# Reading the moving operand of the MLP matmuls in pairs of 64-byte pieces, with the weights at eight places

## The chip, the core and the metric

The kernel runs on one core of a Trainium2 chip. The metric is the time of one execution on the device in microseconds (us). TensorE (PE) multiplies a stationary operand of 128 columns, which a weight load (PEld) brings in, with a moving operand that streams past it, and sums in PSUM. VectorE (DVE) and ScalarE (ACT) read PSUM and write SBUF.

## The reference

An attention with exponential features and then two MLPs over 2304 tokens, one after the other, each 512 to 2048 to 512:

```python
q_p, k_p = (phi(q), phi(k))
...
attn_out = (num / den)
x = np.ascontiguousarray(attn_out.transpose(0, 2, 1, 3)).reshape(B * S, H * D)
h = x @ moe_w_in;  g = np.maximum(0.01 * h, h);             x = g @ moe_w_out
h = x @ moe2_w_in; g = h * np.tanh(np.log1p(np.exp(h)));    x = g @ moe2_w_out
```

(`phi` projects with `w_phi`, subtracts the largest absolute value and takes `exp` of both signs; the softplus of the second MLP is cut at 20.)

## The kernel before

The attention comes first, sixteen pairs of heads one after the other. It leaves X, the transposed activations, in SBUF. Then each MLP runs over five blocks of tokens: two of 512, the 256 left-over tokens, and two more of 512. The function `moe` works on a list `seq` of steps; one step is one block and one 128-wide slice `m` of the hidden layer (two slices for the block of 256 tokens). Sixteen slices `m` make the hidden layer.

In a step, `emit_h` makes the hidden values: four chunks `kk` of the model dimension are summed into a PSUM bank `a`. `leaky` or `mish` turn that bank into the activated values on ACT and DVE, and `emit_o`, two or three steps later, multiplies them into four banks `b`.

Every product is made of three matmuls in the function `three` (lines 83 to 86). A number is split into a high part and a low part, both of type fp32r: high by high, high by low, low by high. Each of the three has a weight load of its own, and the next load runs while the current matmul streams.

What moves and what stays differs by place. In `emit_h` the weights of slice `m` stay (tiles `wh`, `wl` of slice m, part 0) and a window of the activations moves (tiles `wh`, `wl` of the pool `winp`; the trace gives both kinds the same name). In `emit_o` of the first MLP the output weights stay (part 1 of the same tiles) and the activated values `gh`, `gl` move. In `emit_o` of the second MLP it is the other way: 128 columns of `gh` or `gl` stay, and the output weights move. The moving operand is a contiguous stretch of 512 or 256 columns of 4 bytes in each partition, read from the first to the last, and so is the output in PSUM.

Where the tiles lie matters here. The pools stand in SBUF one behind the other. `X` takes 36,864 bytes of a partition and `two` 32, and all tiles of the MLPs behind them have sizes that are multiples of 512 bytes. So every moving and every stationary operand of both MLPs starts at the same place modulo 512, namely 160 bytes past a multiple of 512 (the offsets of chunks and slices are multiples of 512 bytes too). A stationary operand of 128 columns is 512 bytes of each partition.

The order of the instructions is written out by hand (`tc.manual_schedule()`).

Of the kernel before, what the change touches and what calls it, by code (L numbers as in the profile page):

```python
# [10 lines left out]
F32 = mybir.dt.float32  # L11
# [12 lines left out]
def attention_two_mlps_kernel(  # L24
# [17 lines left out]
    P = 128  # L42
    KD = DM // P
    M = DFF // P
# [17 lines left out]
    xp = tc.alloc_tile_pool(name="xp", bufs=1)  # L62
# [7 lines left out]

    X = xp.tile([P, KD, NT], F32, name="X")
    two = xp.tile([P, 1], F32, name="two")[:, 0:1]

    rings = {"a": ps}

    def bank(ring):
        return rings[ring].tile([P, 512], F32, tag=ring, name=ring)
# [2 lines left out]
        nc.scalar.activation(out=hi, in_=src, func=AF.Copy)  # L80
        nc.vector.tensor_tensor(out=lo, in0=src, in1=hi.bitcast(F32), op=ALU.subtract)

    def three(o, wh_, wl_, xh, xl, start=True, stop=True):
        nc.tensor.matmul(out=o, lhsT=wh_, rhs=xh, start=start, stop=False)  # L84
        nc.tensor.matmul(out=o, lhsT=wh_, rhs=xl, start=False, stop=False)  # L85
        nc.tensor.matmul(out=o, lhsT=wl_, rhs=xh, start=False, stop=stop)  # L86
# [6 lines left out]
    class Conv:  # L93
# [45 lines left out]
        def split(self):  # L139

            if self.half is not None:
                u, c = self.half
                self.half = None
                split_w(self.which, u // 2, u % 2, c)()
# [25 lines left out]
        def step(self, *between):  # L170
# [3 lines left out]
            if self.open is not None:  # L174
                u, kind, c, e = self.open
                if kind != "fetch":
                    nc.vector.scalar_tensor_tensor(out=c.bitcast(I32), in0=c.bitcast(I32), scalar=3, in1=e,
                                                   op0=ALU.logical_shift_left, op1=ALU.bitwise_or)
                if kind == "store":
                    scr[self.which, u] = dr.tile([P, DM], F32, name=f"scr{self.which}_{u}")  # L180
                    nc.sync.dma_start(out=scr[self.which, u], in_=c)
                else:
                    after = split_w(self.which, u // 2, u % 2, c)
# [25 lines left out]
    def split_w(which, m, x, src):  # L209

        if x == 0:
            pool = wp0 if m < EARLY else wp
            W[which, m] = [pool.tile([P, 2, KD, P], F32R, tag=f"{t}{m}", name=f"w{t}{m}") for t in "hl"]
        hi, lo = (t[:, x].rearrange("p k f -> p (k f)") for t in W[which, m])
        nc.scalar.activation(out=hi, in_=src, func=AF.Copy)
        return lambda: nc.vector.tensor_tensor(out=lo, in0=src, in1=hi.bitcast(F32), op=ALU.subtract)
# [19 lines left out]
    def split_w2(m, parts=(0, 1)):  # L236
        for x in parts:
            split_w(1, m, x, w_st.pop((m, x)))()
# [12 lines left out]
    with tc.manual_schedule():  # L251
# [112 lines left out]
        def k_proj(i, c):  # L364
            s = st[i]
            if c == 0:
                s["kd"] = ap.tile([P, 2, NM, F], F32, tag="kd", name="kd")
            t = bank("a")
            for j in range(2):
                u = slice((2 * c + j) * P, (2 * c + j + 1) * P)  # L370
                three(t[:, j * 2 * F:(j + 1) * 2 * F], s["kh"][:, u], s["kl"][:, u], wbh, wbl)
            k_guard(t.rearrange("p (n f) -> p n f", f=F), NM, s["kd"][:, c])

        def k_proj_left(i):
            l = lf[i // 2]
            l["kd"] = ap.tile([P, 2, F], F32, tag="kdl", name="kdl", bufs=1)
            t = bank("a")
            three(t[:, 0:2 * F], l["h"][:, 0:P], l["l"][:, 0:P], wbh, wbl)
            k_guard(t[:, 0:2 * F].rearrange("p (n f) -> p n f", f=F), 2, l["kd"])
# [6 lines left out]
        def q_proj(i, c):  # L386
            s = st[i]
            h, o = divmod(c, 2)
            if "qd" not in s:
                s["qd"] = ap.tile([P, 2, S], F32, tag="qd", name="qd")  # L390
                s["qm"] = ap.tile([P, 2, S], F32, tag="qm", name="qm", bufs=1)
            t = bank("a")
            n = HM + (h == o) * LEFT
            c0 = h * (HM + (1 - o) * LEFT)
            d0 = (1 - o) * (HM + h * LEFT)
            f = slice(o * F, (o + 1) * F)
            three(t[:, 0:n], wbh[:, f], wbl[:, f], s["qh"][:, c0:c0 + n], s["ql"][:, c0:c0 + n])
            nc.scalar.activation(out=s["qd"][:, h, d0:d0 + n], in_=t[:, 0:n], func=AF.Copy)  # L398
            half = s.setdefault("half", set())
            half.add(c)  # L400
            if {2 * h, 2 * h + 1} <= half:
                qd, qm = s["qd"][:, h, :], s["qm"][:, h, :]
                nc.gpsimd.partition_all_reduce(qm, qd, P, bass_isa.ReduceOp.absmax)  # L403
# [176 lines left out]
        def emit_h(it):  # L580
            j, ms = it
            a, c0, n = blocks[j]
            hb[it] = bank("a")
            for i, m in enumerate(ms):
                hi, lo = W[a, m]
                for kk in range(KD):
                    three(hb[it][:, i * n:(i + 1) * n], hi[:, 0, kk, :], lo[:, 0, kk, :], win[j][kk][0], win[j][kk][1],
                          start=(kk == 0), stop=(kk == KD - 1))

        def emit_o(it, ds=None):  # L590
            j, ms = it
            a, c0, n = blocks[j]
            gh, gl = gt[it]
            nb = KD if a == 0 else n // P
            if ms[0] == 0:
                acc[j] = [bank("b") for _ in range(nb)]
            for d in ds or range(nb):
                for i, m in enumerate(ms):
                    hi, lo = (x[:, 1] for x in W[a, m])
                    if a == 0:  # L600
                        c = slice(i * n, (i + 1) * n)
                        three(acc[j][d][:, 0:n], hi[:, d, :], lo[:, d, :], gh[:, c], gl[:, c],
                              start=(m == 0), stop=(m == M - 1))
                    else:
                        c = slice(i * n + d * P, i * n + (d + 1) * P)
                        three(acc[j][d], gh[:, c], gl[:, c], hi.rearrange("p k f -> p (k f)"),
                              lo.rearrange("p k f -> p (k f)"), start=(m == 0), stop=(m == M - 1))

        def finish(j, d):
            a, c0, n = blocks[j]  # L610
# [102 lines left out]
        def moe(g):  # L713
            for x in [g, g + 1] if g == jump else [g + 1] if g > jump else [g]:
                if x < len(seq):
                    if x != HEAD:
                        emit_h(seq[x])
                    if seq[x][1][-1] == M - 1 and seq[x][0] + 1 < NB:
                        window(seq[x][0] + 1)
# [13 lines left out]
            if 0 <= g - 2 < len(seq) and seq[g - 2][0] <= last1:  # L733
                j, ms = seq[g - 2]
                emit_o(seq[g - 2])
                if ms[-1] == M - 1:
                    for d in range(KD):
                        finish(j, d)
                if 0 < j < last1:
                    conv2.step()  # L740
                    if conv2.done() and not w_st:
                        load_w2(0)
                if j == last1:
                    m = ms[0]
                    split_w2(m, (0, 1) if m < M - 1 else (0,))
                    if m < M - 1:
                        load_w2(m + 1, (0, 1) if m < M - 2 else (0,))
                    else:
                        load_w2(m, (1,))
                        tail[0] = g + 1  # L750
# [3 lines left out]
            if 0 <= g - 3 < len(seq) and seq[g - 3][0] > last1:  # L754
                j, ms = seq[g - 3]
                if seq[g - 3] == seq[-1]:

                    emit_o(seq[-1], (0, 1))
                    finish(j, 0)
                    finish(j, 1)  # L760
                    for d in (2, 3):
                        for it in seq[-2:]:
                            emit_o(it, (d,))
                        finish(j, d)
                elif seq[g - 3] == seq[-2]:
                    emit_o(seq[-2], (0, 1))
                else:
                    emit_o(seq[g - 3])
                    if ms[-1] == M - 1:
                        done = j  # L770
# [3 lines left out]
        for n in range(PAIRS + 1):  # L774
            attention(n)
        emit_h(seq[HEAD])
        x_t(PAIRS - 1)()
        ap.release()
# [45 lines left out]
```

## Time and profile before

| what | value |
|---|---|
| median of 2 runs | 967.64 us (967.16 to 968.13) |
| profiled execution, span | 964.1 us |
| PE busy | 953.0 us, 99% of the span |
| PEld busy | 813.7 us, 84% |
| DVE busy | 712.7 us, 74% |
| ACT busy | 496.1 us, 51% |
| granted clock of TensorE, mean | 1.000 |

The span runs from the first to the last instruction of the profiled execution; the timed runs are 3.5 us longer, which is work around the span. A matmul's record is longer than the distance to the next matmul's start, because matmuls are pipelined: the busy time of PE says little, and the distance between starts is what counts.

### The profile page before, as it was taken

The page shows a single profiled execution, that of the slowest core. Times are in us where ns is not written, and L with a number is a line of the kernel's source. Part 1 is how long each engine was busy: PE and PEld are TensorE (multiplying, and loading weights), DVE is VectorE, ACT ScalarE, POOL GpSimd, SP SyncE. Part 2 cuts the span into 40 slices and gives each one's busy share as a digit, 9 for nine tenths or more (in the row PEclk, how much of TensorE's full clock was granted, in tenths as well). Part 3 has the DMA queues.
Part 4 walks back from the last instruction along what each step waited for, and adds up shares of the span by engine and source line. Part 5 has one row for each costly group of instructions (what it writes and reads, how often), then busy time and mean ns, then how long its engine had stood idle before and what let it go on. Part 6 is the DMA issues. An engine that isn't in the chain of part 4 may idle for free.

```text
span 964.1 us, 16775 instructions
## 1 busy us (share of the span) xinstructions
PE 953.0 (99%) x6736; PEld 813.7 (84%) x6736; DVE 712.7 (74%) x1269; ACT 496.1 (51%) x850; POOL 68.5 (7%) x36
## 2 busy tenths in 40 slices
PE   8999999999999999999999999999999999999998
PEld 7888999788888899888888888888888988888886
DVE  7999998599656575664344469778878689778875
ACT  6888888455433343332334456455545455445443
POOL 4433433000000000000000000000000000000000
PEclk9999999999999999999999999999999999999999
DMA  7545552354224444443012310001000100001001
GB/s 207 133 120 148 147 137 85 97 167 154 66 88 145 150 140 135 149 138 129 1 44 87 92 62 1 1 1 44 1 1 1 44 1 23 1 1 44 0 1 44
DMA packets 68205, 72.98 MB, mean 76 GB/s; under 512 B 27168, under 2 KB 52640, under 8 KB 68128
## 3 DMA queue, kind: packets, MB, share of 16 engines
q1 hardware_dynamic: 67392, 71.52, 24.2%
q8 instruction: 53, 0.87, 0.4%
q10 hardware_dynamic: 736, 0.39, 0.1%
q14 instruction: 24, 0.20, 0.1%
HBM read 57.48 MB, written 14.42 MB: 75 GB/s over the span
## 4 chain that ended last, share of the span: by engine, by line
PE 93%; DVE 4%; ACT 2%; issue 0%; POOL 0%; DMA 0%; ACTq 0%; DVEq 0%
PE a L84 15%; PE a L85 15%; PE a L86 15%; PE b L84 14%; PE b L86 14%; PE b L85 14%; PE outs L443 2%; PE kvp L420 2%; PE a L336 1%; PE xt L468 1%; DVE qd L407 1%; DVE mx L360 1%; DVE kd L361 1%; PE kvp L423 0%; POOL qm L403 0%
## 5 line engine op out<-in xcount | busy, mean ns | idle before, releaser
L84 PE MATMUL a<-wh,wh 128*128 128x512 f32 (+1 forms) x640 | 235.7, 368 | 0.0
L85 PE MATMUL a<-wl,wh 128*128 128x512 f32 (+1 forms) x640 | 235.4, 368 | 0.0
L86 PE MATMUL a<-wh,wl 128*128 128x512 f32 (+1 forms) x640 | 235.4, 368 | 0.0
L84 PEld LDWEIGHTS a<-wh,wh 128*128 128x128 f32 x640 | 120.7, 189 | 20.7 <-issue 0.4
L85 PEld LDWEIGHTS a<-wl,wh 128*128 128x128 f32 x640 | 120.6, 188 | 20.2
L86 PEld LDWEIGHTS a<-wh,wl 128*128 128x128 f32 x640 | 120.7, 189 | 20.0
L656 DVE TENSOR_TENSOR gl<-g,gh 128x512 fp32r<-128x512 f32 x72 | 49.9, 693 | 110.2 <-ACT gh L653 110.2
L84 PE MATMUL b<-gh,wh 128*128 128x512 f32 (+1 forms) x320 | 117.8, 368 | 0.8 <-ACT X L478 0.8
L85 PE MATMUL b<-gl,wh 128*128 128x512 f32 (+1 forms) x320 | 117.7, 368 | 0.0
L86 PE MATMUL b<-gh,wl 128*128 128x512 f32 (+1 forms) x320 | 117.7, 368 | 0.0
L86 PE MATMUL b<-wh,gl 128*128 128x512 f32 x288 | 112.2, 389 | 0.0
L85 PE MATMUL b<-wl,gh 128*128 128x512 f32 x288 | 112.2, 389 | 0.0
L84 PE MATMUL b<-wh,gh 128*128 128x512 f32 x288 | 112.1, 389 | 0.0
L653 ACT ACTIVATE gh<-g 128x512 fp32r<-128x512 f32 x72 | 45.5, 632 | 116.0 <-PE b L86 109.5
L678 ACT ACTIVATE gh<-u 128x512 fp32r<-128x512 f32 x72 | 45.5, 632 | 70.5 <-PE b L85 63.8
L652 DVE TENSOR_TENSOR g<-g,a 128x512 f32<-128x512 f32 x72 | 49.4, 686 | 41.2 <-ACT g L649 38.5
L403 POOL PARTITION_ALL_REDUCE qm<-qd x32 | 68.3, 2182 | 90.4 <-ACT qd L398 87.0
L705 ACT ACTIVATE r<-e,two 128x512 f32<-128x512 f32 x72 | 51.6, 717 | 36.3 <-DVE e L690 36.3
L84 PEld LDWEIGHTS b<-gh,wh 128*128 128x128 f32 x320 | 60.3, 189 | 11.0 <-ACT X L478 0.9
L85 PEld LDWEIGHTS b<-gl,wh 128*128 128x128 f32 x320 | 60.4, 189 | 9.9
L86 PEld LDWEIGHTS b<-gh,wl 128*128 128x128 f32 x320 | 60.3, 188 | 9.9
L674 ACT ACTIVATE e<-a 128x512 f32<-128x512 f32 x72 | 43.0, 597 | 47.8 <-PE a L86 26.5
(115 smaller groups left out, 1610.7 us busy)
## 6 DMA issues: line engine op xcount, KB each, us to landing
stage<-in_moe_w_in_dram SPq DMA_DIRECT2D x32, 512.0 KB, 3.8
stage<-in_moe_w_out_dram SPq DMA_DIRECT2D x32, 512.0 KB, 3.6
scr<-c SPq DMA_DIRECT2D x37, 256.0 KB, 2.0
wstage<-scr SPq DMA_DIRECT2D x32, 256.0 KB, 3.9
qn<-in_q_dram SPq DMA_DIRECT2D x16, 256.0 KB, 4.5
vmain<-in_v_dram SPq DMA_DIRECT2D x32, 128.0 KB, 3.8
kn<-in_k_dram SPq DMA_DIRECT2D x15, 256.0 KB, 4.4
out_dram<-X SPq DMA_DIRECT2D x15, 256.0 KB, 2.2
```

Of the source, the lines that this page charges most:

```text
L84: nc.tensor.matmul(out=o, lhsT=wh_, rhs=xh, start=start, stop=False)
L85: nc.tensor.matmul(out=o, lhsT=wh_, rhs=xl, start=False, stop=False)
L86: nc.tensor.matmul(out=o, lhsT=wl_, rhs=xh, start=False, stop=stop)
L403: nc.gpsimd.partition_all_reduce(qm, qd, P, bass_isa.ReduceOp.absmax)
L420: nc.tensor.matmul(out=both[r, h, a, :], lhsT=s["kp"][a][:, h, t, r], rhs=s["vm"][:, h, t, :], start=(a == 0 and h == 0 and t == 0), stop= ...
L443: nc.tensor.matmul(out=g[r, u // 2, u % 2, h], lhsT=s["qp"][a][:, h, q0 + r.start:q0 + r.stop], rhs=s["kv"][:, 2 * h + a], start=(a == 0), ...
L652: nc.vector.tensor_tensor(out=g, in0=g, in1=h, op=ALU.max)
L653: nc.scalar.activation(out=hi, in_=g, func=AF.Copy)
L656: nc.vector.tensor_tensor(out=lo, in0=g, in1=hi.bitcast(F32), op=ALU.subtract)
L674: nc.scalar.activation(out=e0, in_=h0, func=AF.Exp)
L678: nc.scalar.activation(out=hi2, in_=u2, func=AF.Copy)
L705: nc.scalar.activation(out=r0, in_=e0, func=AF.Ln, bias=two)
```

## The change

In all matmuls of the two MLPs the moving operand and the output are read and written in another order of columns. The 512 (or 256) columns are cut into two halves, and each half into pieces of 16 columns, that is 64 bytes. The order is: the last piece of the first half, the last piece of the second half, the piece before the last of the first half, and so on to the first pieces. For 512 columns the two pieces of a pair are 1024 bytes apart, for 256 columns 512 bytes. Output column and input column go together, so that the values in PSUM lie where they lay before. The matmuls of the attention keep their order.

Besides, a tile `even` of 32 bytes that nobody uses stands in front of the pool of the windows, and a tile `pad` of 64 bytes that nobody uses stands in front of the weight tiles of each slice `m` from 1 to 15. With them windows and activated values start 192 bytes past a multiple of 512, and the weights of slice `m` start 192 + 64 m bytes past one, modulo 512: eight places, each the place of two of the sixteen slices.

No instruction is added, removed or moved on any engine; the instructions stand in the same order as before.

```diff
     two = xp.tile([P, 1], F32, name="two")[:, 0:1]
+    xp.tile([P, 8], F32, name="even")
...
-    def three(o, wh_, wl_, xh, xl, start=True, stop=True):
+    def down(x):
+        return x.rearrange("p (t s g) -> p s t g", t=2, g=16)[:, ::-1]
+
+    def three(o, wh_, wl_, xh, xl, start=True, stop=True, back=False):
+        if back:
+            o, xh, xl = (down(x) for x in (o, xh, xl))
...
             pool = wp0 if m < EARLY else wp
+            if m and which == 0:
+                pool.tile([P, 16], F32, name=f"pad{m}")
...
-                          start=(kk == 0), stop=(kk == KD - 1))
+                          start=(kk == 0), stop=(kk == KD - 1), back=True)
...
-                              start=(m == 0), stop=(m == M - 1))
+                              start=(m == 0), stop=(m == M - 1), back=True)
...
-                              lo.rearrange("p k f -> p (k f)"), start=(m == 0), stop=(m == M - 1))
+                              lo.rearrange("p k f -> p (k f)"), start=(m == 0), stop=(m == M - 1), back=True)
```

## Rows read from the trace of the kernel before

**Rows 1.** Page, part 1: busy us, share of the span, instructions.
```profile
PE 953.0 (99%) x6736; PEld 813.7 (84%) x6736; DVE 712.7 (74%) x1269; ACT 496.1 (51%) x850; POOL 68.5 (7%) x36
```
**Rows 2.** Page, part 4: the chain that ended last, by engine and line.
```profile
PE 93%; DVE 4%; ACT 2%; issue 0%; POOL 0%; DMA 0%; ACTq 0%; DVEq 0%
```
**Rows 3.** Groups by line and shape, PE: count | busy us, mean ns | idle before.
```profile
L84 PE MATMUL a<-wh,wh 128*128 128x512 f32 x512 | 199.6, 390 | 0.0
...
L84 PE MATMUL b<-wh,gh 128*128 128x512 f32 x288 | 112.1, 389 | 0.0
L84 PE MATMUL b<-gh,wh 128*128 128x512 f32 x256 | 99.7, 390 | 0.8 <-ACT X L478 0.8
...
L84 PE MATMUL a<-wh,wh 128*128 128x256 f32 x128 | 36.2, 283 | 0.0
L420 PE MATMUL kvp<-vmain,kp 128*64 128x65 f32 x1024 | 35.3, 221 | 0.0
...
L84 PE MATMUL b<-gh,wh 128*128 128x256 f32 x64 | 18.1, 283 | 0.0
...
L423 PE MATMUL kvp<-vleft,lp 128*64 128x130 f32 x128 | 12.6, 275 | 0.0
...
L468 PE MATMUL xt<-ident,xn 128*128 128x128 f32 x64 | 9.9, 277 | 0.0
```
**Rows 4.** Timeline of PE, 600 to 640 us: start us, duration us, instruction.
```profile
599.83 0.39 PE L86 MATMUL a<-wh,wl 128*128 128x512 f32 x1
...
639.95 0.39 PE L86 MATMUL a<-wh,wl 128*128 128x512 f32 x1
```
**Rows 5.** Timeline of PE, 731.6 to 734.4 us, end of one step.
```profile
731.37 0.28 PE L84 MATMUL a<-wh,wh 128*128 128x256 f32 x1
...
732.69 0.28 PE L86 MATMUL a<-wh,wl 128*128 128x256 f32 x1
732.81 0.40 PE L84 MATMUL b<-wh,gh 128*128 128x512 f32 x1
733.05 0.40 PE L85 MATMUL b<-wl,gh 128*128 128x512 f32 x1
733.28 0.39 PE L86 MATMUL b<-wh,gl 128*128 128x512 f32 x1
733.51 0.40 PE L84 MATMUL b<-wh,gh 128*128 128x512 f32 x1
733.74 0.39 PE L85 MATMUL b<-wl,gh 128*128 128x512 f32 x1
733.97 0.39 PE L86 MATMUL b<-wh,gl 128*128 128x512 f32 x1
734.20 0.39 PE L84 MATMUL b<-wh,gh 128*128 128x512 f32 x1
```
**Rows 6.** Timeline of PE, 340.2 to 342.2 us, the block of 256 tokens begins.
```profile
341.02 0.28 PE L84 MATMUL a<-wh,wh 128*128 128x256 f32 x1
341.13 0.28 PE L85 MATMUL a<-wl,wh 128*128 128x256 f32 x1
```
**Rows 7.** Timeline of PE, 65.6 to 66.6 us, transposes of the attention.
```profile
65.95 0.60 PE L468 MATMUL xt<-ident,xn 128*128 128x128 f32 x4
```
**Rows 8.** Groups by line and shape, weight loads: busy us, mean ns.
```profile
L84 PEld LDWEIGHTS a<-wh,wh 128*128 128x128 f32 x640 | 120.7, 189 | 20.7 <-issue 0.4
...
L468 PEld LDWEIGHTS xt<-ident,xn 128*128 128x128 f32 x64 | 7.3, 140 | 0.9
```
**Rows 9.** Windows: busy us (instructions) of PE, PEld, DVE, ACT, POOL; granted clock.
```profile
600.00:700.00 100.00, 100.00 (x442) 82.80 (x442) 81.57 (x137) 50.27 (x80) 0.00 (x0) 1.00 0.03 11
800.00:900.00 100.00, 100.00 (x442) 82.79 (x442) 84.04 (x143) 51.84 (x83) 0.00 (x0) 1.00 0.03 12
```

## The prediction

> **What bounds the kernel now.** I read the page first: PE is busy 99% of the span, DVE 74%, ACT 51% [rows 1], and the chain that ended last lies 93% on PE [rows 2]. So an edit counts only if it shortens the stream of matmuls. The groups by shape then say how many there are. Of 512 columns there are three lines each of 512, 288 and 256 matmuls, 3 x 1056 = 3168; of 256 columns three lines each of 128 and 64, 576 in all [rows 3]. PE waits for nothing in front of them but 0.8 us in one place [rows 3].
>
> The mean of a matmul in these groups (389 and 283 ns) is not its price, since matmuls overlap. The price is the distance between starts, and the timeline has it. Between 599.83 and 639.95 us stand 178 matmuls of 512 columns, so 177 steps in 40.12 us: 226.67 ns each [rows 4]. In the block of 256 tokens twelve steps take 1.44 us: 120.0 ns each [rows 5]. The difference is 106.7 ns for 256 columns, or 0.4167 ns for one. That is one column in each cycle of 2.4 GHz, and the granted clock is 1.00 there [rows 9]. Taken off, 226.67 - 512 x 0.4167 and 120.0 - 256 x 0.4167 both leave 13.3 ns. So every MLP matmul pays 13.3 ns over its columns, whatever its length, 3744 x 13.3 ns = 49.9 us in all. The MLP matmuls take 3168 x 226.67 + 576 x 120.0 ns = 787 us of the span. The columns themselves can't be made fewer; the 13.3 ns is all that this change can touch.
>
> **Is the 13.3 ns fixed?** Three rows say no. Where 512 columns follow on 256, five steps from 732.81 to 733.97 us take 232 ns each, and then the step is back near 227, with the same instructions, shapes and tiles; and the records of those matmuls last 0.40 us where the settled ones last 0.39 [rows 5]. The first matmul of the 256-token block takes a step of 0.11 us where the settled one is 0.12 [rows 6]. And four transposes of 128 columns with a weight load each go by steps of (0.60 - 0.277) / 3 us = 107.7 ns [rows 3, 7]. Plain fp32 columns go at half the speed (from 65 columns, 221 ns, to 128, 277 ns [rows 3], it is 0.8 to 0.9 ns a column), and 128 x 0.833 = 106.7 leaves 1 ns; allowing for the two decimals I take 2 ns. So the surplus is from 2 ns up to 19 (232 - 213.3) and depends on how two things stand in time. The only other work of PE at that time is the next weight load.
>
> Where both MLPs' operands start at the same place modulo 512, a moving stream passes all eight 64-byte places of 512 bytes in 8 x 16 x 0.4167 = 53 ns. The load of fp32r weights lasts 189 ns against 140 for plain fp32 [rows 8]. If the plain one reads a column in a cycle (53 ns), then the other reads its 128 columns in 53 + 49 = 102 ns, close to two cycles each; that is an estimate. So the weights walk through the same eight places at half the speed, 13.3 ns in each, and the moving stream runs into them in each load and waits for them to leave. This is my reading of the 13.3 ns, and not shown: no row names a place in SBUF.
>
> **The change, part by part.** *The order of the pieces.* A pair of pieces lies at the same place modulo 512 and takes 2 x 16 x 0.4167 = 13.3 ns, just as long as the weights stay at one. The moving stream then walks at the weights' speed, from the last place to the first. If weights are read from the last column on, both go the same way at the same pace and meet only if they start at the same place. Then the surplus falls from 13.3 ns to the floor of 2 ns.
>
> *The eight places.* The distance between both streams takes each of the eight values for two of sixteen slices. Started one after the other, they overlap at two neighbouring values of eight, and there the moving stream waits once, between 0 and 13.3 ns, 6.7 on average, after which it stays behind. So the mean surplus is 2 + 2/8 x 6.7 = 3.7 ns and the saving 9.7 ns: 3744 x 9.7 ns = 36.2 us. The tile `even` puts windows on a multiple of 64 bytes and costs nothing; no instruction is added, and the attention's own tiles all shift by the same amount.
>
> *What the pieces may cost.* A moving operand in pieces stands nowhere in this trace. The nearest row is an output in two runs: L423 writes 130 columns in two runs of 65 and lasts 275 ns, the transposes with 128 in one run 277 [rows 3]; so one break can't be seen. I take zero for each; the end on the other side is one cycle for each of 32 pieces, 13.3 ns for 512 columns and 6.7 for 256, together 46 us.
>
> *What comes next.* With PE 4% faster DVE's load in the second MLP goes from 84 to 88 us in 100, ACT's from 52 to 54 [rows 9]. Both still keep up; if the steps fell to their bare columns, 213.3 ns, DVE would be at 89. So the gain isn't given back there.
>
> **Sum.** 964.1 - 36.2 = 927.9 us of span, with the 3.5 us around it 931.4. The ends of this case: at no surplus at all 964.1 - 49.9 + 3.5 = 917.7; at a floor of 1 ns in each place, 12.3 x 3744 = 46.1, 921.5; with the floor no better than the 0.113 to 0.114 us that the one short step may be (some 6.7 ns of surplus [rows 6]) and the two bad places as now, 5 ns saved, 949. I put its range at 921 to 949.
>
> **Rivals.**
>
> *No collision at all: 967 us.* The 13.3 ns may be what it costs to swap in new weights, and the unsettled steps some other slip in time. For it speaks that the surplus is the same at 512 and 256 columns and in every place of 3744 matmuls; against it that the transposes, with a load each, hardly have it [rows 7], and that it changes with no change of instruction [rows 5, 6]. Chance 0.18. The Trainium skill ("SBUF — State Buffer", "Who interferes with whom") gives PE two independent read ports, one for the moving operand and one for the weights, and says that PE never waits on anyone. By that rule reads can't collide and the time stays at 967.6; rows 5 don't bear it out, as they show the same matmul at two prices, though they don't show that it is SBUF that it waits for.
>
> *Weights are read from the first column on: 950 us.* Nothing in the trace shows the direction. Then the streams meet head on. The first meeting costs the moving stream 0 to 13.3 ns, 6.7 on average, after which both step at the same moment and pass each other. Surplus 8.7, saving 4.6 x 3744 = 17.4 us, time 950.2. Chance 0.12.
>
> *The pieces cost a cycle each: 1014 us.* If the address walk loses a cycle at each jump, on the read or on the write into PSUM, the stream pays 46 us, and if nothing else is gained the time is 967.6 + 46 = 1014. It decides from 0.33 ns a piece on, where it eats the forecast saving (36.2 / 46 x 0.4167), and reaches 2% slower at 0.17 ns without that saving. For it speaks that every MLP operand of now is one run and no row has 32; against it the two runs of L423. Chance 0.13. The Trainium skill ("PSUM — Partial Sum Buffer", "Specifications (TRN2)") says that any non-contiguous access pattern in PSUM slows matmuls significantly, with lines of 8 bytes; here each piece fills eight such lines. Taken as it stands the rule gives this rival, a time above 1000 us; the row of L423, with its two runs, doesn't show it.
>
> **How the numbers follow.** Forecast 0.57 (921 to 949), no collision 0.18 (965 to 969), head on 0.12 (941 to 960), pieces dear 0.13 (975 to 1014). The predicted time is the forecast's, 931.4. A range of 921 to 949 holds little over half, so it must reach to the case without effect: 921 to 969 leaves out the dear pieces and a little of the low end. About 2%, 948 to 987 us, is what a measurement of this kernel tells from no change. Faster: nearly all of the forecast and a third of head on, 0.60. Slower: most of the dear pieces, 0.12. The rest, 0.28, is within.
>
> **What would show it.** In the profile after, the timeline of 512 columns should step by 215 to 217 ns in most slices and by up to 227 in a quarter of them, that of 256 columns by 109 to 113; the step should change with the slice `m`, in step with the eight places. If it is 226.7 everywhere, the surplus is no collision. If it is 226.7 + 13 in every slice, the pieces are dear. Steps that are all alike but lower would say that the places don't matter and the order alone does. DVE's waits on PE should shrink and none of PE's on DVE appear; if PE waits for `gl` in the second MLP, part of the gain went there. I am wrong in the size if more than two places in eight are bad, and in the direction if jumps within the operand cost anything at all that adds up over 32.

## The result: 1.3% slower, and the profile after

The changed kernel takes 980.19 us (979.71 to 980.67, 2 runs) against 967.64 us; the ratio is 1.013, with an interval of 1.0101 to 1.016. The forecast was 931.4 us, and 980 lies outside its range of 921 to 969. The profiled execution has a span of 977.5 us, 13.4 more than before. It took 979.71 us, 2.2 more than its span, as in all later runs; the 3.5 us that the prediction adds to the span of before is 1.3 us too much, because that time and that span come from different executions.

The page after, part 1, answers to [rows 1]: the busy times of DVE and ACT are as they were, and what is longer is PE's.

```profile
PE 965.9 (99%) x6736; PEld 812.0 (83%) x6736; DVE 713.2 (73%) x1269; ACT 495.7 (51%) x850; POOL 68.5 (7%) x36
```

The groups by line and shape of the changed kernel, PE (count | busy us, mean ns of one | idle before), answer to [rows 3]; lines 84 to 86 are now 90 to 92:

```profile
L90 PE MATMUL a<-wh,wh 128*128 128x512 f32 x512 | 201.5, 394 | 0.0
...
L90 PE MATMUL b<-gh,wh 128*128 128x512 f32 x256 | 100.9, 394 | 0.8 <-ACT X L486 0.8
...
L90 PE MATMUL a<-wh,wh 128*128 128x256 f32 x128 | 35.8, 280 | 0.0
```

One matmul of 512 columns is 4 ns longer than before, one of 256 columns 3 ns shorter, and nothing waits in front of them that did not wait before. The windows (busy us and instructions of PE, PEld, DVE, ACT, POOL; granted clock) answer to [rows 9]: fewer matmuls in the same 100 us, at the same clock.

```profile
600.00:700.00 100.00, 100.00 (x434) 80.93 (x433) 80.70 (x136) 49.55 (x79) 0.00 (x0) 1.00 0.03 11
```

The timeline of PE (start us, duration us) shows what one mean hides. From each line to the next that is shown stand twelve matmuls: the output matmuls of slice 5, the hidden matmuls of slice 8, the output matmuls of slice 6.

```profile
208.29 0.40 PE L90 MATMUL b<-gh,wh 128*128 128x512 f32 x1
...
211.13 0.40 PE L90 MATMUL a<-wh,wh 128*128 128x512 f32 x1
...
213.92 0.39 PE L90 MATMUL b<-gh,wh 128*128 128x512 f32 x1
...
216.67 0.39 PE L90 MATMUL a<-wh,wh 128*128 128x512 f32 x1
```

The steps are 2.84, 2.79 and 2.75 us by twelve: 236.7, 232.5 and 229.2 ns, where the kernel before had 226.7 in every place [rows 4]. So the step does depend on the slice, as forecast, but at 512 columns every slice is worse. In the block of 256 tokens twelve matmuls take 1.41 us, 117.5 ns each, against 120.0 [rows 5]:

```profile
345.80 0.28 PE L90 MATMUL a<-wh,wh 128*128 128x256 f32 x1
...
347.21 0.40 PE L90 MATMUL b<-gh,wh 128*128 128x512 f32 x1
```

Over all MLP matmuls the mean distance between starts is 231.5 ns at 512 columns (before 226.8, the unsettled ones included, five or six steps above 270 ns left out) and 117.8 at 256 (119.8). 3168 x 4.7 - 576 x 2.0 ns = 13.7 us, close to the 13.4 us between the spans: the MLP matmuls are all of it.

### The profile page after: what moved, and what is told of

Same layout as the page of the kernel before. It is cut to its first block, busy times and chain, and to the rows that moved or that the text cites. A ratio compares the mean times of both kernels' runs of the same rounds, so it can differ in the third digit from the quotient of the medians.

```text
span 977.5 us, 16836 instructions
## 1 busy us (share of the span) xinstructions
PE 965.9 (99%) x6736; PEld 812.0 (83%) x6736; DVE 713.2 (73%) x1269; ACT 495.7 (51%) x850; POOL 68.5 (7%) x36
## 4 chain that ended last, share of the span: by engine, by line
PE 93%; DVE 3%; ACT 2%; issue 0%; POOL 0%; DMA 0%; ACTq 0%; DVEq 0%
PE a L90 15%; PE a L92 15%; PE a L91 15%; PE b L92 14%; PE b L90 14%; PE b L91 14%; PE outs L451 2%; PE kvp L428 2%; PE a L344 1%; PE xt L476 1%; DVE qd L415 1%; PE kvp L431 0%; DVE mx L368 0%; POOL qm L411 0%; DVE kd L369 0%
```

## The experiments

Two theories stood after the result. *Dear jumps*: the order avoids the collisions, but each jump from one 64-byte piece to the next costs part of a cycle or more. *Meeting streams*: jumps are free, and the moving stream still meets the weight load, in another rhythm than the prediction thought. "Surplus" is the step less the bare columns (213.3 ns at 512, 106.7 at 256).

The table has the step of each run from one place of the timeline, 600 to 640 us, where all matmuls have 512 columns: first start, last start, number of matmuls, and their mean distance. The edits and expectations follow below it.

| run | time us | first and last start, matmuls | step ns |
|---|---|---|---|
| before | 967.64 | 599.83, 639.95, 178 | 226.7 |
| changed kernel | 980.19 | 599.65, 639.77, 174 | 231.9 |
| places alone | 979.95 | 599.74, 639.85, 175 | 230.5 |
| order alone | 988.65 | 599.72, 639.86, 173 | 233.4 |
| only the moving operand in pieces | 979.66 | 599.64, 639.99, 175 | 231.9 |
| only the output in pieces | 980.28 | 599.63, 639.97, 176 | 230.5 |
| all weights 64 bytes further | 984.03 | 599.72, 639.93, 174 | 232.4 |
| all weights 128 bytes further | 984.82 | 599.64, 639.96, 174 | 233.1 |
| jumps over the same places | 968.15 | 599.80, 639.92, 178 | 226.7 |
| last piece first, no pairs | 985.85 | 599.78, 639.91, 173 | 233.3 |
| pairs, first pair first | 1008.02 | 599.63, 639.97, 169 | 240.1 |
| loads and moving apart | 1002.44 | 599.78, 639.83, 169 | 238.4 |
| loads and moving together | 1003.19 | 599.65, 639.93, 170 | 238.3 |
| moving place by place | 1006.00 | 599.74, 639.97, 169 | 239.5 |
| half loads | 974.90 | 599.68, 639.90, 176 | 229.8 |
| load from the first place | 977.82 | 599.64, 639.85, 175 | 231.1 |
| load from the fourth place | 977.49 | 599.77, 639.98, 175 | 231.1 |
| moving stays at one column | 928.99 | 599.66, 639.87, 187 | 216.2 |
| both stay at one column | 930.91 | 599.76, 639.99, 187 | 216.3 |

### The two parts of the change apart

Places alone, from the changed kernel:

```diff
-        if back:
-            o, xh, xl = (down(x) for x in (o, xh, xl))
```

> The spare tiles stand as in the changed kernel, every operand is read in one run from the first column on. Dear jumps: without jumps nothing is dear, so the steps are those of before on average, 226.7 ns and 120.0 ns, 960 to 970 us; places may shift single slices by some ns. Meeting streams: the step differs from slice to slice with the place, in a pattern that repeats after four places (256 bytes), by up to 10 ns either way, 945 to 985 us. Neither (a fixed price for each matmul): 226.7 ns in every slice, 967.6 us.

979.95 us (4 runs), ratio 1.0125 (1.0108 to 1.0142). So the spare tiles alone, with the order of before, make the kernel as slow as the whole change. The mean step by slice, over all blocks, shows a pattern that repeats after four slices, that is 256 bytes, not eight (slices 4 to 7 stand for the rest):

```
                                slice 4   slice 5   slice 6   slice 7   slice 8   slice 9
hidden matmuls                    229.2     233.2     232.1     229.0     229.0     233.2
output matmuls, first MLP         228.3     233.2     233.0     233.1     228.3     233.2
output matmuls, second MLP        227.2     230.6     231.6     233.1     226.9     230.6
```

In slices 4 and 8 both operands stand at the same place. Their output matmuls are the nearest to the old 226.7; in the hidden row slice 7 has as low a mean, and none is clearly below 226.7. The means hold unsettled steps: where hidden slice 8 and the output matmuls of slice 4 follow each other, the 18 steps between these two lines take 226.7 ns each. So the 32 bytes of the tile `even`, by which all operands are shifted there, cost nothing by themselves.

```profile
608.53 0.39 PE L89 MATMUL a<-wl,wh 128*128 128x512 f32 x1
...
612.61 0.39 PE L89 MATMUL b<-wl,gh 128*128 128x512 f32 x1
```

The fixed price for every matmul is out.

Order alone, from the changed kernel:

```diff
-    xp.tile([P, 8], F32, name="even")
...
-            if m and which == 0:
-                pool.tile([P, 16], F32, name=f"pad{m}")
```

> The order of the pieces as in the changed kernel, without the spare tiles, so that all operands start at the same place again. Dear jumps: the pieces cost what they cost at any place, about 980 us, steps of 229 to 233 ns alike in all slices. Meeting streams: one step for all slices of a kind, near what the changed kernel has at equal places (233 ns in the hidden matmuls, 228 in the output matmuls), 975 to 985 us; the spread over slices is gone under both, so this run alone gives the share of the places in the 12.5 us.

The timeline of PE (start us, duration us), first and last of 173 matmuls:

```profile
599.72 0.40 PE L90 MATMUL b<-wl,gh 128*128 128x512 f32 x1
...
639.86 0.40 PE L91 MATMUL b<-wh,gl 128*128 128x512 f32 x1
```

988.65 us (4 runs), ratio 1.0217 (1.0202 to 1.0232), one mean step of 233.4 ns (40.14 us by 172) for all slices and kinds; most single steps are 231 and 236 ns in turn. So both parts lose, by 12.2 and 20.9 us against the 967.72 us of the kernel before beside them, and together they lose 12.5: they don't add up, and the eight places take back part of what the order costs.

### Jumps, on either side

```diff
-            o, xh, xl = (down(x) for x in (o, xh, xl))
+            xh, xl = (down(x) for x in (xh, xl))
```

> The moving operand is read in pieces, the output is written in one run, so the columns of the results stand in another order; the places are those of the changed kernel. If the reading side decides (meeting streams, or dear jumps in the read): steps as in the changed kernel, 980 us. If jumps in the PSUM write are dear: the steps fall, and the meetings that the order avoids are gained, 930 to 965 us.

```diff
-            o, xh, xl = (down(x) for x in (o, xh, xl))
+            o = down(o)
```

> The output is written in pieces, the moving operand is read in one run, so the columns of the results stand in another order; places as in the changed kernel. If the reading side decides: the steps are those of the run with the places alone. If jumps in the PSUM write are dear: 12 to 19 us above that run (0.4 to 0.5 ns for each of 32 pieces would be 46 us).

With the moving operand alone in pieces 979.66 us, as the changed kernel; with the output alone 980.28, as the places alone. The order in which PSUM is written decides nothing here. The reading side was left, and for it a run with as many jumps, over the old sequence of places (from the kernel before; here and below the lines that hand `back` to `three` are left out):

```diff
+    def down(x):
+        return x[:, 0:320].rearrange("p (a b) -> p a b", b=80)[:, :, 0:16].unsqueeze(1).to_broadcast([P, 8, 4, 16])
...
+        if back and xh.shape[1] == 512:
+            o = o.rearrange("p (e a b) -> p e a b", e=8, a=4)
+            xh, xl = (down(x) for x in (xh, xl))
```

> The kernel before, but each moving operand of 512 columns is read in 32 pieces of 64 bytes, each 320 bytes behind the last and after four of them back at the first, so that the places modulo 256 bytes follow each other as in one run; most columns of the results are left out and others stand there eight times. The output is written in one run; operands of 256 columns stay as they were. Dear jumps: what the order alone cost, 6.7 ns, or more for each matmul of 512 columns, 985 to 1015 us. Meeting streams with a period of 256 bytes: 226.7 ns, 965 to 970 us. A period of 512 bytes: another steady step, 226 to 236 ns.

Its timeline of PE (start us, duration us), first and last of 178 matmuls:

```profile
599.80 0.39 PE L90 MATMUL b<-wh,gh 128*128 128x512 f32 x1
...
639.92 0.39 PE L90 MATMUL a<-wh,wh 128*128 128x512 f32 x1
```

40.12 us by 177 is 226.67 ns, the step of before to the last digit, and 968.15 us against 968.18 of the kernel before beside it. These 32 jumps are free; dear jumps is out. Of the moving operand's walk this run kept only the sequence of places modulo 256 bytes.

### The place of the weights

```diff
+            if m == 0 and which == 0:
+                pool.tile([P, 16], F32, name="shift")
```

> The kernel before with one spare tile of 64 bytes in front of the first weights, so that weights and the rest lie one place apart in all slices alike. Places decide: every slice has the step that the slices one place apart have in the run with the places alone (233.2 ns in the hidden and the first output matmuls; 233.1 in the second output matmuls, which lie three places apart), 984 to 990 us. The change of place is what costs (each new place unsettles the streams, a lasting one does not): the steps settle at 226.7 ns, 965 to 970 us.

The same with `[P, 32]`:

> The same with 128 bytes. Places decide: 232 ns in all slices, 980 to 987 us. The change of place costs: 226.7 ns, 965 to 970 us.

The timeline of PE with 64 bytes, first and last of 174 matmuls, 40.21 us by 173:

```profile
599.72 0.39 PE L84 MATMUL a<-wh,wh 128*128 128x512 f32 x1
...
639.93 0.39 PE L86 MATMUL a<-wh,wl 128*128 128x512 f32 x1
```

984.03 and 984.82 us. The first has 233.3 ns in all slices of the hidden and the first MLP's output matmuls and 230.5 in the second's (233.1 was expected there; the places alone have 230.6 in slice 5, where the second MLP's operands lie as far apart); the second has 232 to 234 everywhere. So a lasting distance costs as much as a changing one: the place decides, and equal places with one run, the state before, was the best of the distances tried for 512 columns. For 256 columns it was not: with 64 bytes the hidden matmuls of that block took 116.1 ns instead of 119.8.

### The order of the moving operand

```diff
-        return x.rearrange("p (t s g) -> p s t g", t=2, g=16)[:, ::-1]
+        return x.rearrange("p (s g) -> p s g", g=16)[:, ::-1]
```

> Equal places; the moving operand and the output run from the last piece of 64 bytes to the first, one after the other, no pairs. Dear jumps: as many jumps as with pairs, so the same 233.4 ns, 985 to 990 us. Meeting streams: the pairs halve the pace of the moving stream and this run does not, so the step differs from 233.4; if weights are read from the last column on it passes them less often than one run upwards does, below 226.7 ns and 930 to 965 us; if they are read from the first column on, more often, above 227 ns.

985.85 us and 233.3 ns, the step of the pairs at equal places (233.4). The direction's expected gain did not come, and halving the pace made no difference either at 512 columns (at 256 it is 117.8 ns against 120.7 with pairs).

```diff
-        return x.rearrange("p (t s g) -> p s t g", t=2, g=16)[:, ::-1]
+        return x.rearrange("p (t s g) -> p s t g", t=2, g=16)
```

> The changed kernel with its eight places, but the pairs run from the first to the last. Weights read upwards at half the pace (the premise of the prediction with the direction turned round): the streams walk side by side, and in three of four places the step falls to 215 to 218 ns at 512 columns, 930 to 945 us. Weights not at half the pace, or the wait not set by where both streams stand: steps of 228 to 237 ns that differ from place to place as in the changed kernel, 975 to 990 us.

The timeline of PE, first and last of 169 matmuls:

```profile
599.63 0.40 PE L92 MATMUL a<-wh,wl 128*128 128x512 f32 x1
...
639.97 0.40 PE L92 MATMUL a<-wh,wl 128*128 128x512 f32 x1
```

240.1 ns, and the mean by slice lies between 239.6 and 240.3 in all sixteen slices of all three kinds: with this order the place of the weights doesn't matter at all. This is the first run that meeting streams, as the prediction had them, can't explain.

### Is the weight load the partner?

The load is kept at one place, and the moving operand is read place by place (all operands start at equal places, with the tile `even` and without the tiles `pad`):

```diff
+    def down(x):
+        return x.rearrange("p (b s g) -> p s b g", s=4, g=16)
+    def at(x, col=48):
+        return x[:, col:col + 1].to_broadcast([P, P])
...
+        if back:
+            wh_, wl_ = at(wh_), at(wl_)
+            o, xh, xl = (down(x) for x in (o, xh, xl))
```

> A measurement of the floor: all operands at equal places, each weight load takes one column of its weights 128 times, from the fourth place of 256 bytes alone, and the moving operand is read place by place (all pieces of the first place, then of the second, the fourth place last); output columns alike; so each result row is the product with one column of weights. Meeting streams between moving operand and weight load: they are apart while the load runs, and the step falls to 215 to 217 ns at 512 columns; with 256 columns the last place comes within the load, 110 to 125 ns; about 925 to 940 us. No meeting between these two (the wait is inside the moving stream, or a fixed price of the load): 226 to 235 ns, 965 to 990 us.

With `col=0`:

> The same as the run with loads and moving operand apart, but the one column of weights lies in the first place, where the moving operand begins. Meeting streams: the moving operand waits for the load at the start of each matmul or shares the place with it, so the step is clearly above that of the run apart, by 10 to 100 ns at 512 columns. No meeting: the same step in both runs.

And the same order with the loads as they were:

> A correct kernel: the moving operand is read place by place (eight pieces, 256 bytes apart, of each of four places), equal places, weights as before. Meeting streams: each load passes the place of the moving operand twice in its course and either stream waits one piece each time; if the moving stream waits, two to four pieces of 6.7 ns, 227 to 240 ns, 967 to 1010 us; if the load waits, nothing, 216 ns and 930 to 940 us. Dear jumps (already out by the run with jumps over the same places): 233 ns or more.

The timelines of PE, first and last matmul, of the run apart:

```profile
599.78 0.40 PE L95 MATMUL b<-wl,gh 128*128 128x512 f32 x1
...
639.83 0.40 PE L95 MATMUL b<-wl,gh 128*128 128x512 f32 x1
```

and of the run together:

```profile
599.65 0.40 PE L96 MATMUL a<-wh,wl 128*128 128x512 f32 x1
...
639.93 0.40 PE L94 MATMUL b<-wh,gh 128*128 128x512 f32 x1
```

238.4 and 238.3 ns: where the load stands makes no difference here (at 256 columns the steps are 118.2 and 116.7), and with whole loads (239.5) it is little worse. Meeting streams, in the form that the prediction gave it, falls with these runs. (The records of loads of one column are as long as those of whole ones, 188 to 189 ns; whether such a load reads the memory 128 times, no run shows.) The moving operand in one run, with loads from one column:

```diff
+        if back:
+            wh_, wl_ = (x[:, 0:1].to_broadcast([P, P]) for x in (wh_, wl_))
```

> The kernel before, the moving operand in one run, but each weight load takes its first column 128 times, so it reads one place alone, the one where the moving operand begins; each result row is the product with that column. The place of the load matters by where both stand: a step other than 226.7 ns, and another one than in the run with the load from the fourth place. Only the order of the moving operand matters: 226.7 ns in both.

> The same with column 48, which lies 192 bytes further. The place of the load matters: a step that differs from the run with the first column by one or more pieces of 6.7 ns. Only the order of the moving operand matters: 226.7 ns in both.

The timelines of PE, first and last of 175 matmuls, with the load from the first place:

```profile
599.64 0.39 PE L86 MATMUL b<-wh,gh 128*128 128x512 f32 x1
...
639.85 0.39 PE L86 MATMUL a<-wh,wh 128*128 128x512 f32 x1
```

and from the fourth:

```profile
599.77 0.40 PE L88 MATMUL b<-wh,gl 128*128 128x512 f32 x1
...
639.98 0.40 PE L88 MATMUL a<-wh,wl 128*128 128x512 f32 x1
```

Again equal, 231.1 ns both, and neither expectation came: not 226.7, and not two different steps. Without a walk of the load the moving stream still has a surplus of 17.8 ns, more than with the walk at equal places; at 256 columns it is 113.4 ns. And a load of half the length beside the first of three matmuls:

```diff
-        nc.tensor.matmul(out=o, lhsT=wh_, rhs=xl, start=False, stop=False)
+        nc.tensor.matmul(out=o[0:h], lhsT=wh_[:, 0:h], rhs=xl, start=False, stop=False)
```

> The kernel before, but the second of each three matmuls uses 64 columns of its weights instead of 128, so its load is half as long; half of the high by low products are left out. That load runs beside the first matmul of the three. The load is the partner of the wait: the step of the first matmul (the one that the short load runs beside) falls by about half of its 13.3 ns, to some 220 ns, the two others stay near 226.7. The wait lies in the moving stream alone, or is a fixed price: 226.7 ns for all three.

974.9 us; the short loads' records last 135 ns in place of 188, and the three steps are 228.9, 230.5 and 230.0 ns, none lower than before at 512 columns. The surplus does not shrink with the load. (The run also leaves out half of the output partitions of one matmul in three.)

The last two runs took away the walk of the moving operand:

```diff
+        if back:
+            xh, xl = (x[:, 0:1].to_broadcast([P, x.shape[1]]) for x in (xh, xl))
```

> The kernel before, weights loaded as they are, but the moving operand is its first column, read 512 or 256 times, so the moving stream visits one place alone; all columns of a result are alike. The wait comes from the moving stream's walk over the places: the step falls to 215 to 217 ns at 512 columns and 109 at 256, 920 to 935 us. The wait comes from the load, or is part of changing weights: 225 to 235 ns, 113 to 120. The moving stream meets the load: the load passes its place twice, one or two waits of 6.7 ns, 220 to 229 ns.

With the loads from one column too:

> The same, and each load takes its first column 128 times, so that neither stream walks. Either stream's walk is the cause: 215 to 217 ns at 512 columns. The change of weights itself costs: 227 ns or more, as in the run with the walking moving operand and the load from the first place (231 ns).

The timeline of PE with the moving operand at one column, first and last of 187 matmuls (the last row of the table has both at one column):

```profile
599.66 0.38 PE L88 MATMUL b<-wh,gl 128*128 128x512 f32 x1
...
639.87 0.38 PE L88 MATMUL b<-wh,gl 128*128 128x512 f32 x1
```

216.2 and 216.3 ns; 928.99 and 930.91 us. With whole, walking loads and a moving operand that stays, the surplus is 2.9 ns. So the 10.4 ns above it belong to the moving operand's reading, and changing weights costs none of it. Whether one column read over and over is fetched anew each time, no run shows, so the reading and the walk over places are not told apart. At 256 columns the step is 111.6 ns, a surplus of 4.9, where 109 was expected.

### A version that beats both

The gain for 256 columns in the run with 64 bytes was tried by itself:

```diff
+            w0 = 0 if n == MAIN else 48
...
-                hi = winp.tile([P, MAIN], F32R, tag="wh", name="wh")[:, 0:n]
-                lo = winp.tile([P, MAIN], F32R, tag="wl", name="wl")[:, 0:n]
+                hi = winp.tile([P, MAIN], F32R, tag="wh", name="wh")[:, w0:w0 + n]
+                lo = winp.tile([P, MAIN], F32R, tag="wl", name="wl")[:, w0:w0 + n]
```

> A correct kernel: the kernel before, with the window of the blocks of 256 tokens 192 bytes further in its tile, so that in their 384 hidden matmuls the weights lie one place ahead of the moving operand, as in the run with all weights 64 bytes further, where these matmuls took 116.1 ns instead of 119.8. The places carry over: 384 x 3.7 ns = 1.4 us less, 966.2 us, a ratio of 0.9985. They do not carry over to a single group of matmuls: 967.6 us.

965.91 us (11 runs) against 967.43: ratio 0.9983, 0.9974 to 0.9992. Its group of hidden matmuls of 256 columns (count | busy us, mean ns) has 280 ns where [rows 3] has 283, and the mean distance between their starts is 116.6 ns against 119.8:

```profile
L84 PE MATMUL a<-wh,wh 128*128 128x256 f32 x128 | 35.8, 280 | 0.0
```

So the place of one group of matmuls sets its own step, and the effect can be used, if only by 1.5 us here (1.4 were expected).

## Why the prediction was wrong

**What held.** PE's stream bounds the kernel, the surplus is not fixed, and it differs from slice to slice. The floor was put at 2 ns by the transposes [rows 7]; the moving operand at one column has 2.9 at 512 columns and 4.9 at 256. The Trainium skill ("TensorE: Matmul & The Clock Gate", "Back-to-back issue gap") gives N / 2.4 + 2.5 ns as the gap of an isolated matmul at full clock, an estimate of 215.8 at 512 columns, and about 131 ns a matmul for a stream of loads and matmuls in pairs. The 216.2 here agrees with the first, the 226.7 of this kernel with neither, and no run of this case came near the second. The surplus was large enough for the forecast saving, too: 38.4 us (928.99 against 967.38), though in a kernel that leaves out all but one column of the moving operand, so no run shows that a kernel with the right results can have it. And DVE and ACT kept up there: in the groups by line the longest wait of the MLP matmuls is 0.8 us, for ACT, as before.

**The step that failed** is the first under the order of the pieces: "The moving stream then walks at the weights' speed, from the last place to the first. If weights are read from the last column on, both go the same way at the same pace and meet only if they start at the same place." That the surplus is a meeting of the moving stream with the weight load was called a reading and not shown, and then carried the whole sum. The pairs upwards cost 240 ns at every place of the weights, loads apart and together cost the same, and loads from one place leave a surplus of 17.8 ns. The sum itself, 3744 x 9.7 ns, rested on nothing else. Its two terms measured: the order was to cut the surplus from 13.3 to 2 ns, and alone it raised it to 20.1 (233.4 less 213.3); the places were to cost 1.7 ns in the mean, and alone they raised the mean step at 512 columns from 226.8 to 231.0, by 4.2. The sign that the prediction named for being wrong in the direction, jumps that cost, did not come either.

**The places.** They were priced at two bad places of eight, against six good ones. There are four, not eight, and the state before, equal places and one run, is a good one: with the operand in one run all other places cost 2 to 7 ns more at 512 columns. The prediction took the 13.3 ns of before for the bad case, because all operands start alike; a steady step in 3744 matmuls could as well have been the best case, and it said nothing on which of the two it was.

**The rivals.** No collision at all: out, since the mean steps of the slices go from 226.9 to 233.2 ns with the places alone. By the Trainium skill ("SBUF — State Buffer", "Who interferes with whom") PE has two independent read ports and waits on no one; the runs apart and together, and those with the load at two places, agree with that in that the load's place made no difference (238.4 and 238.3, 231.1 and 231.1 ns), and the shifts of all weights don't, 232.4 and 233.1 against 226.7 ns. Head on: it forecast 950 and gave the same mechanism, so it falls too. Dear pieces had the right sign for a wrong reason, and that its range, 975 to 1014, holds the measured time is luck: 32 jumps over the same places cost nothing, and neither do outputs in pieces. The rule of the Trainium skill ("PSUM — Partial Sum Buffer", "Specifications (TRN2)") that any non-contiguous pattern in PSUM slows matmuls significantly does not hold for pieces of 64 bytes: 980.28 us with them and 979.95 without.

**What stays open.** The surplus hangs on the moving operand's reading and, where it is read whole, on the order in which it visits four places of 64 bytes; what it waits for there is not settled, so the cause of the loss stays open below this level. Shifting the weights (226.7 to 233), halving a load (to 229.8 in the mean of three) and taking the load's walk away (to 231.1) all change it, none removes it, and with pairs upwards the weights' place changes nothing. So the load takes part in the rhythm but was not shown to be what is waited for. With pairs upwards, and place by place, the surplus grows with the length (13.4 and 11.1 ns at 256 columns, 26.7 and 26.2 at 512), while the load is the same at both; that speaks for waits within the moving stream in these two orders, and no run takes the load out to show it. Whether waits arise between one matmul's reads and the next one's was not tried. A rival that the prediction does not list, that the moving operand waits for DVE's or ACT's traffic, the traces do not bear out: in the kernel before the 370 steps of 512 columns in which neither was busy have a mean of 226.8 ns, as have the 2320 in which one or the other was busy throughout; in the changed kernel they are 231.3 and 231.5.

## What to carry to other kernels

A steady surplus in every instruction shows that the rhythm is the same everywhere, not that it is a bad one: before breaking it up, move one operand by one place and look at the step. Where a mechanism is only a reading of two rows, the cheap test is to take one of the two partners away (here an operand of one column, read over and over): it would have shown in one run that the moving side carries the 10 ns. And a mean step by place and by kind, from the starts in the timeline, tells more than the time of the run.

## What the runs showed of the hardware that was not expected

Several mean steps are whole multiples of 6.67 ns, the time of 16 columns or one piece of 64 bytes: 226.67 is 34 of them (before, and with jumps over the same places), 233.3 is 35 (order alone, last piece first, and most slices with the weights 64 bytes further), 240.1 is 36 (pairs upwards), where the bare columns are 32. It is no rule: the steps of 238.4, 231.1 and 216.2 ns lie between the multiples, and with the order alone 233.3 is a mean of 231 and 236. The pattern over places repeats after 256 bytes. And the surplus need not be the same at both lengths: one run at equal places has 13.3 ns at 512 and at 256 columns, pairs upwards 26.7 and 13.4, loads from one column 17.8 and 6.7.
